# Products of a constant tile at the start, eight places for raw weight blocks, and four items' exponentials taken from PSUM

## The chip, the cores and the metric

One core of a Trainium2 chip runs the whole program. TensorE multiplies, VectorE (DVE), ScalarE (ACT) and GpSimd (POOL) do the element-wise work, and SyncE (SP) issues the DMA transfers. The metric is the device time of one execution in microseconds; the kernel before takes 992.88 us, the median of 3 runs.

## What is computed

Attention with positive random features, followed by a feed-forward block. The inputs are q, k and v of shape 8 x 8 x 576 x 64 (batch, heads, sequence, head size), omega of 128 x 64, w_in of 512 x 2048 and w_out of 2048 x 512, all float32 (q is drawn 4.675 times wider than k).

```python
def phi(x):
    proj = np.einsum('bhsd,md->bhsm', x, omega)
    sq = np.sum(x * x, axis=-1, keepdims=True) / 2.0
    h = proj - sq
    h = h - np.max(h, axis=-1, keepdims=True)
    return np.exp(h) / np.sqrt(m)
q_p, k_p = (phi(q_s), phi(k_s))
kv = np.einsum('bhsm,bhsd->bhmd', k_p, v)
z = np.sum(k_p, axis=2)
num = np.einsum('bhsm,bhmd->bhsd', q_p, kv)
den = np.einsum('bhsm,bhm->bhs', q_p, z)[..., None] + 1e-06
...
h = x @ w_in
sp = np.where(h > 20.0, h, np.log1p(np.exp(np.minimum(h, 20.0))))
g = h * np.tanh(sp)
return (g @ w_out).astype(np.float32)
```

q_s and k_s are q and k over the fourth root of 64, and x is the attention output laid out as 4608 tokens of 512. Since the square term is the same for all features of a row, the subtraction of the row's maximum takes it away.

## The kernel before

**Items.** The attention is cut into 68 items. A key item (`k_task`) is one batch and two of its heads: the keys times omega (`pk`, nine tiles of 128 x 128), the row maxima, the exponentials `e`, and their product with the values (`pkv`). A query item (`q_task`) is 128 tokens of all eight heads: `pq`, maxima, exponentials, a transpose, and the product with the keys' result (`pn`). The order begins with the four key items of batch 0 (items 0 to 3), four query items (4 to 7), the four key items of batch 1 (8 to 11) and the fifth query item (12). These thirteen are computed in float32 throughout ("whole" in the code); all later ones split each operand into two float16 parts and make three products. `features` (L294 to L344) does what both kinds share: a PSUM tile from the pool `ps_a` (four places) for each group of up to four tiles, a reduction for the maxima, and the exponentials into a buffer `e` (two places).

**Maxima and exponentials.** For the items numbered below 9, ACT takes the exponential straight from PSUM, one instruction for each 128 x 128 tile, with the negated maximum as bias (L332). From item 9 on, VectorE subtracts the maxima from PSUM into `e` (L336) and ACT then takes one exponential over all of `e` (L342). Which it is follows from the table `ROLE` by the entry `sub="AD"`: A below item 9, D from there.

**Weights.** w_in comes as eight raw blocks of 1 MB of 64-bit words (a float32 pair each, so that the low and high halves can be taken apart), fetched by `fetch_w` (L137 to L149). A `w_task` (L160 to L182) then unpacks each: a Prelu on ACT (L169), a shift (L170), an or (L174) and a reduction for the block's largest value (L177) on VectorE. When all eight maxima are there, the scale follows (`am_w`, L190), and `w_split` (L198 to L209) makes the two float16 parts. The raw blocks of w_in take turns in four places inside the tile `wo`, so block 4 to 7 can be fetched only once block 0 to 3 is unpacked; w_out's blocks go to two places in `wo` and to buffers of the tag "g" (four places), which the first key loads and the feed-forward activations also use. The split of w_out later overwrites `wo`.

**Feed-forward.** Tokens go through in 18 chunks of 256. Chunk 0 is done in float32 on the unpacked, unscaled weights (`ph` at L609, then `po` at L669); the later ones take three float16 products (L609, L652).

**What sets the order.** The program is written as generators on an agenda; a step counter runs on, and a task resumes at its due step. `FIRST` holds the steps at which the first 18 items start, `WIS` those of the eight w_in blocks, `WOS` those of w_out, and `PREL` the loads that are issued before everything else. Each engine then executes its own queue in order, and so does SP with the transfers that it issues. A scheduling layer places the instructions into the queues, so a change in one place can shift neighbours on all engines. Transfers that wait for a free place hold up those behind them on SP.

Of the kernel before, what the change touches and what calls it, by code (L numbers as in the profile page):

```python
# [9 lines left out]
F16 = mybir.dt.float16  # L10
F32 = mybir.dt.float32
# [3 lines left out]
AF = mybir.ActivationFunctionType  # L15
# [14 lines left out]
def tile_kernel(  # L30
# [10 lines left out]
    nc = tc.nc  # L41
    P = 128
    NT, D, H, _ = qT.shape
    B, HP, _, _, S = kT.shape
# [12 lines left out]
    const = ctx.enter_context(tc.tile_pool(name="const", bufs=1))  # L57
    sb = ctx.enter_context(tc.tile_pool(name="sb", bufs=2))
    ps_h = ctx.enter_context(tc.tile_pool(name="ps_h", bufs=2, space=PSUM))
    ps_o = ctx.enter_context(tc.tile_pool(name="ps_o", bufs=2, space=PSUM))  # L60
    ps_a = ctx.enter_context(tc.tile_pool(name="ps_a", bufs=4, space=PSUM))

    act, dve, pool = nc.scalar, nc.vector, nc.gpsimd
# [19 lines left out]
    lnt = const.tile([P, 1], F32, name="lnt")  # L83
    dve.memset(lnt, LNT)

    ident = const.tile([P, P], F32, name="ident")
    make_identity(nc, ident)

# [48 lines left out]
    def fetch_w(n, i, dma):  # L137
        src = w_src[n](i)


        at = i % 4 if n == 0 else {7: 0, 6: 1, 3: 0}.get(i)
        if at is not None:
            if n == 0 and i >= 4:
                must(1, "w", 0, i - 4)
            raw = wo_t[:, 2 * at:2 * at + 2].rearrange("p a b c -> p (a b c)").bitcast(I64)
        else:
            raw = sb.tile([P, BW], I64, tag="g", name=f"raw{i}", bufs=GB)
        dma.dma_start(out=raw.rearrange("p (a b) -> p a b", b=src.shape[2]), in_=src)
        return raw  # L149
# [8 lines left out]
    def w_task(i, name):  # L158

        n = 0 if name == "wi" else 1  # L160
        raw = loaded.pop(f"w{n}_{i}", None) or fetch_w(n, i, w_dma)
        yield W_LOAD
        word = raw.bitcast(I32).rearrange("p (n two) -> p n two", two=2)
        low, high = word[:, :, 0], word[:, :, 1]
        dst = flat32(slots[w_at(n, i)])
        di = dst.bitcast(I32)
        with behind((AN, AO)[n][i]):
            m = high.bitcast(F32)
            act.activation(m, m, AF.Prelu, scale=2.0 ** -112, alpha=-(2.0 ** 32))  # L169
            dve.tensor_single_scalar(out=di, in_=low, scalar=29, op=ALU.logical_shift_right)  # L170
        yield W_GAP
        did("w", n, i)
        with behind((AN, AO)[n][i]):
            dve.scalar_tensor_tensor(  # L174
                out=di, in0=high, scalar=3, in1=di, op0=ALU.logical_shift_left, op1=ALU.bitwise_or
            )
            dve.tensor_reduce(  # L177
                out=wmax[n][:, i:i + 1], in_=dst, axis=AX.X, op=ALU.max, apply_absolute_value=True
            )
# [37 lines left out]
    def must(n, *key):  # L217
        assert done.get(key, 0) >= n, key
# [57 lines left out]
    kv = {}  # L276
# [5 lines left out]
    def fetch(load, name, tag="af", bufs=2):  # L282
        f = sb.tile([D, load.shape[1] * load.shape[2]], F32, tag=tag, name=f"f{name}", bufs=bufs)
        nc.sync.dma_start(out=f.rearrange("d (a b) -> d a b", b=load.shape[2]), in_=load)
        return f

    def in_parts(f, name, nth):

        ks = sb.tile([P, f.shape[1]], F16, tag="as", name=f"s{name}", bufs=2)
        cast(by("hi", nth), ks[0:D], f)  # L290
        yield gap("hi", name)
        rest(by("lo", nth), ks[D:P], f, ks[0:D])
        yield gap("lo", name)
        return (ks, om[:, 1, :]), (ks, om[:, 0, :])  # L294

    def features(load, tiles, name, nth, whole):

        f = loaded.pop(name, None) or fetch(load, name)  # L300
        yield gap("load", name)
        if whole:

            terms = ((f, om_f[0:D]),)
        else:
            terms = yield from in_parts(f, name, nth)
        n = sum(len(g) for g in tiles)
        by_act = by("sub", nth) is act
        e = sb.tile([P, n, M], F32, tag="ae", name=f"e{name}", bufs=2)
        mx = sb.tile([P, n], F32, tag="mx", name=f"mx{name}")  # L310
        pps, lo = [], 0
        for g in tiles:
            pp = ps_a.tile([P, 4, M], F32, tag="a", name=f"p{name}_{lo}")
            for i, parts in enumerate(g):
                for rows, o in parts:
                    for j, (left, right) in enumerate(terms):
                        nc.tensor.matmul(  # L317
                            out=pp[rows, i, :], lhsT=left[:, o:o + rows.stop - rows.start],
                            rhs=right, start=j == 0, stop=j == len(terms) - 1,
                        )  # L320
            pps.append((pp, lo, lo + len(g)))
            lo += len(g)
        yield 1
        for pp, lo, hi in pps:
            m = hi - lo
            sub = dve.tensor_reduce(  # L326
                out=mx[:, lo:hi], in_=pp[:, :m, :], axis=AX.X, op=ALU.max, negate=by_act
            )
            if by_act:
                assert whole  # L330
                for i in range(m):
                    last = act.activation(  # L332
                        e[:, lo + i, :], pp[:, i, :], AF.Exp, bias=mx[:, lo + i:lo + i + 1]
                    )
            else:
                sub = dve.tensor_tensor(  # L336
                    out=e[:, lo:hi, :], in0=pp[:, :m, :],
                    in1=mx[:, lo:hi].unsqueeze(2).broadcast_to([P, m, M]), op=ALU.subtract,
                )
        yield gap("exp", name)  # L340
        if not by_act:
            last = act.activation(e, e, AF.Exp, bias=0.0 if whole else lnt)  # L342
        anchors[nth] = (last.ins, sub.ins)
        return e  # L344

# [19 lines left out]
    def k_task(nth, b, hp):  # L365
        if hp == 0:
# [7 lines left out]
            [[(rows, S + t * P)] for t in range(4)],  # L374
        ]
        e = yield from features(kT[b, hp], tiles, f"k{b}_{hp}", nth, b < KF)
        dst = kv[b][:, 2 * hp:2 * hp + 2]
        steps = [[(4 * j + i, 5 * j + i) for i in range(5)] for j in range(2)]
# [59 lines left out]
    def q_task(nth, t):  # L438
# [3 lines left out]
        rows = slice(0, P)  # L442
        tiles = [[[(rows, (4 * g + i) * P)] for i in range(4)] for g in range(2)]
        e = yield from features(qT[t], tiles, f"q{t}", nth, t < QF)
        if t < QF:
            yield from q_first(nth, t, e, off)
# [241 lines left out]
    w_dma = nc.sync  # L688

    FIRST = (0, 1, 2, 3, 4, 4, 9, 9, 19, 21, 24, 27, 32, 36, 43, 58, 59, 68)  # L690
    WIS = (4, 5, 6, 7, 9, 11, 12, 13)
    WOS = (28, 27, 26, 25, 24, 23, 22, 21)
    WI0, FF0, V0, V1 = 0, 17, 0, 16
    W_LOAD, W_GAP, PRIO = 1, 1, 400
# [3 lines left out]

    W_LO = ('dddddddd', 'dddddddd')
    W_HI = ('aaaaaaaa', 'aaaaaaaa')  # L700
    PREL = "k0 k2 k1 k3 q0 q1 w0 v w1 w2 w3"
    KF, QF = 2, 5
    GAP0 = {'load': 1, 'exp': 0, 'kv': 1}
    GAP = {'load': 3, 'hi': 1, 'lo': 2, 'exp': 1, 'kv': 2}

    ROLE = dict(hi="AA", lo="PP", sub="AD", kp="AA", kplo="DD", v="DD", vlo="PP", kv="AA", x="AD", xlo="DP", h="DD", h0="DD", gm="DD", g="DA", glo="PD")
    NE, CE = 9, 3
    ENG = {"A": act, "D": dve, "P": pool}

    def gap(what, name):  # L710
        if name in ("k0_0", "k0_1", "k0_2", "k0_3", "q0", "q1"):
            return GAP0[what]
        return GAP[what]
# [5 lines left out]
    def by(role, nth):  # L719
        return ENG[ROLE[role][nth >= NE]]  # L720

    def by_c(role, c):
        if c == 0 and role[0] == "h":
            return act
        return ENG[ROLE[role][c >= CE]]

# [6 lines left out]
    def start(gen, after=0):  # L733
        agenda.append([slot[0] + after, gen])
# [24 lines left out]
    for t in range(NT):  # L759
        last = (t * P + P - 1) // S  # L760
# [29 lines left out]

    for what in PREL.split():
        i = int(what[1:] or 0)
        if what[0] == "k":
            loaded[f"k0_{i}"] = fetch(kT[0, i], f"k0_{i}", *(("af", 2) if i < 2 else ("g", GB)))
        elif what[0] == "q":
            loaded[f"q{i}"] = fetch(qT[i], f"q{i}", "xT", 3)
        elif what[0] == "v":
            for hp in range(HP):
                loaded[f"v0_{hp}"] = fetch_v(0, hp)
        else:  # L800
            loaded[f"w0_{i}"] = fetch_w(0, i, nc.sync)
# [3 lines left out]
    for i in range(NB):  # L805
        start(w_task(i, "wi"), WIS[i])
    for i in reversed(range(1, NB)):
# [83 lines left out]
```

## Time and profile before

| | us |
|---|---|
| median of 3 runs | 992.88 |
| lowest, highest | 992.82, 995.17 |
| the profiled execution | 983.8 |
| its span, first to last instruction | 982.0 |

The page's second part cuts the span into 40 slices and gives the busy tenths of each engine (9 is 90% or more), the granted TensorE clock, and the DMA engines' share; a slice is 24.6 us.

```profile
PE   7999998889999999999999999999999999999998
DVE  4579979688576565656556654655555645211110
ACT  3368656757687777787766875787776776232230
PEclk9999999999999999999999999999999999999999
DMA  9376423542352245223422246322421034200000
```

VectorE is lightly used in the first slices and nearly full from the third to the seventh; the DMA engines are full in the first. In the rows of the timeline that the prediction shows, a row gives the start, the length, the engine, the line, the operation, out<-in, the form, and the number of instructions merged into it; in brackets stands the idle time ahead of it and what ended that. A float32 product counts as two records on TensorE.

### The profile page before, as it was taken

How to read it: one execution, taken by the hardware profiler on the slowest of the kernel's cores; microseconds unless marked ns; L12 is line 12 of the kernel's file. 1: busy time of each engine (PE TensorE's matmuls, PEld its weight loads, DVE VectorE, ACT ScalarE, POOL GpSimd, SP SyncE). 2: the span in 40 equal slices, each digit the busy share in tenths (PEclk: the TensorE clock that was granted, in tenths of full speed). 3: DMA queues.
4: the chain of work that ended last, by engine and by line, in shares of the span. 5: the costliest groups of instructions: out<-in, count | busy, mean ns of one | idle time of the engine just before them, and what ended most of it. 6: DMA issues, size and time to landing. Idle time of an engine off the chain costs nothing.

```text
span 982.0 us, 19120 instructions
## 1 busy us (share of the span) xinstructions
PE 958.3 (98%) x8144; PEld 692.1 (70%) x8144; DVE 552.4 (56%) x974; ACT 625.8 (64%) x783; POOL 219.1 (22%) x135
## 2 busy tenths in 40 slices
PE   7999998889999999999999999999999999999998
PEld 6988775567767777777777777777767777666663
DVE  4579979688576565656556654655555645211110
ACT  3368656757687777787766875787776776232230
POOL 0000013234333322332222332332232230000000
PEclk9999999999999999999999999999999999999999
DMA  9376423542352245223422246322421034200000
GB/s 291 119 246 216 144 57 70 101 86 82 74 122 69 60 96 106 67 55 99 94 62 58 61 102 100 68 57 66 89 67 42 25 76 86 44 22 12 12 11 33
DMA packets 122245, 82.21 MB, mean 84 GB/s; under 512 B 102832, under 2 KB 102960, under 8 KB 122160
## 3 DMA queue, kind: packets, MB, share of 16 engines
q1 hardware_dynamic: 122160, 80.99, 33.1%
q8 instruction: 64, 1.05, 0.4%
q14 instruction: 21, 0.17, 0.1%
HBM read 46.37 MB, written 9.44 MB: 57 GB/s over the span
## 4 chain that ended last, share of the span: by engine, by line
PE 72%; DMA 0%; ACT 0%; DVE 0%; issue 0%; ACTq 0%; SPq 0%
PE po L652 32%; PE ph L609 30%; PE pk L317 3%; PE pq L317 2%; PE pn L468 2%; PE pkv L418 2%; DMA qp<-qn 0%; DVE qn L77 0%; ACT eq L342 0%; ACT qn L68 0%; ACT o L68 0%; ACTq L68 0%; SPq L454 0%
## 5 line engine op out<-in xcount | busy, mean ns | idle before, releaser
L609 PE MATMUL ph<-xT,w 128*128 128x256 f16 (+1 forms) x3392 | 409.8, 277 | 1.0 <-ACT g L68 1.0
L652 PE MATMUL po<-wo,g 128*128 128x512 f16 x1632 | 373.8, 379 | 0.0
L609 PEld LDWEIGHTS <-w 128*128 128x128 f16 x3264 | 317.3, 98 | 59.2 <-issue 0.7
L652 PEld LDWEIGHTS <-g 128*128 128x128 f16 x1632 | 155.6, 98 | 163.6 <-issue 0.4
L628 ACT ACTIVATE h<-ph,us 128x512 f32<-128x512 f32 (+3 forms) x184 | 101.0, 574 | 190.5 <-PE ph L609 189.6
L79 DVE SCALAR_TENSOR_TENSOR g<-h,us,g 128x1024 f16<-128x1024 f32 (+3 forms) x92 | 113.9, 1253 | 119.6 <-ACT g L68 119.3
L77 POOL TENSOR_TENSOR sq<-fq,sq 64x1024 f16<-64x1024 f32 x31 | 71.4, 2303 | 201.0 <-issue 87.5
L77 POOL TENSOR_TENSOR sk<-fk,sk 64x1152 f16<-64x1152 f32 x24 | 60.5, 2522 | 125.4 <-ACT sk L68 27.0
L326 DVE TENSOR_REDUCE mxq<-pq 128x4 f32<-128x512 f32 x72 | 46.8, 683 | 53.2 <-PE pq L317 53.2
L77 POOL TENSOR_TENSOR xs<-x,xs 128x512 f16<-128x512 f32 x32 | 42.4, 1324 | 142.3 <-ACT h L628 56.4
L68 ACT ACTIVATE g<-h,us 128x1024 f16<-128x1024 f32 (+3 forms) x80 | 72.5, 932 | 1.2
L628 ACT ACT_TABLE_LOAD x56 | 71.8, 1283 | 1.0
L342 ACT ACT_TABLE_LOAD x56 | 71.8, 1283 | 1.0
L326 DVE TENSOR_REDUCE mxk<-pk 128x4 f32<-128x512 f32 (+1 forms) x96 | 50.4, 550 | 36.3 <-PE pk L317 36.0
L77 DVE TENSOR_TENSOR qn<-eq,qn 128x1024 f16<-128x1024 f32 x31 | 42.4, 1366 | 48.6 <-ACT qn L68 48.4
L77 DVE TENSOR_TENSOR kp<-ek,kp 128x1152 f16<-128x1152 f32 x24 | 37.2, 1550 | 19.2 <-ACT kp L68 19.2
L77 POOL TENSOR_TENSOR vb<-vf,vb 128x640 f16<-128x640 f32 x24 | 39.8, 1662 | 26.8 <-DVE vb L70 18.4
L68 ACT ACTIVATE o<-po,us 128x512 f32<-128x512 f32 (+1 forms) x38 | 25.9, 681 | 30.2 <-PE po L652 30.1
L342 ACT ACTIVATE eq<-eq,lnt 128x1024 f32<-128x1024 f32 x31 | 35.6, 1149 | 13.6 <-DVE eq L336 13.1
L265 DVE TENSOR_REDUCE vmx<-vf 128x1 f32<-128x640 f32 x32 | 25.6, 814 | 30.1 <-DMA vf<-in_vL_dram 30.1
L336 DVE TENSOR_TENSOR ek<-pk,mxk 128x512 f32<-128x512 f32 (+1 forms) x81 | 42.2, 549 | 0.4
L336 DVE TENSOR_TENSOR eq<-pq,mxq 128x512 f32<-128x512 f32 x64 | 41.2, 680 | 0.0
(112 smaller groups left out, 928.2 us busy)
## 6 DMA issues: line engine op xcount, KB each, us to landing
vf<-in_vL_dram SPq DMA_DIRECT2D x32, 325.0 KB, 3.3
fk<-in_kT_dram SPq DMA_DIRECT2D x32, 288.0 KB, 3.7
fq<-in_qT_dram SPq DMA_DIRECT2D x36, 256.0 KB, 3.5
out_dram<-o SPq DMA_DIRECT2D x36, 256.0 KB, 2.3
wo<-in_w_in_dram SPq DMA_DIRECT2D x8, 1024.0 KB, 10.3
raw<-in_w_out_dram SPq DMA_DIRECT2D x5, 1024.0 KB, 5.9
wo<-in_w_out_dram SPq DMA_DIRECT2D x3, 1024.0 KB, 7.6
xT<-xs SPq DMA_TRANSPOSE x34, 3.1
```

Of the source, the lines that this page charges most:

```text
L68: act.activation(out, in_, AF.Copy, scale=scale)
L77: eng.tensor_tensor(out=out, in0=in_, in1=hi, op=ALU.subtract)
L79: eng.scalar_tensor_tensor(out=out, in0=in_, scalar=scale, in1=hi, op0=ALU.mult, op1=ALU.subtract)
L265: dve.tensor_reduce(out=mx[:, hp:hp + 1], in_=vt[hp][:, :, 0:D], axis=AX.XY, op=ALU.max, apply_absolute_value=True,)
L317: nc.tensor.matmul(out=pp[rows, i, :], lhsT=left[:, o:o + rows.stop - rows.start], rhs=right, start=j == 0, stop=j == len(terms) - 1,)
L326: sub = dve.tensor_reduce(out=mx[:, lo:hi], in_=pp[:, :m, :], axis=AX.X, op=ALU.max, negate=by_act)
L336: sub = dve.tensor_tensor(out=e[:, lo:hi, :], in0=pp[:, :m, :], in1=mx[:, lo:hi].unsqueeze(2).broadcast_to([P, m, M]), op=ALU.subtract,)
L342: last = act.activation(e, e, AF.Exp, bias=0.0 if whole else lnt)
L418: nc.tensor.matmul(out=pkv[:, j, :], lhsT=kp[:, x, t, :], rhs=vv[:, y, u, :], start=i == 0, stop=i == len(mm) - 1,)
L609: nc.tensor.matmul(out=ph[:, i, :], lhsT=wi(a, k, f) if c else wi0(k, f), rhs=xT[c][:, y, k, :] if c else xT0()[:, k, :], start=n == 0, st ...
L628: act.activation(h[:, :, lo:hi], ph[:, :, lo:hi], AF.Mish, scale=us[:, 0:1])
L652: nc.tensor.matmul(out=po[i], lhsT=gT[c, gr][:, a, f % FG, i * P:(i + 1) * P], rhs=wo(y, f), start=f == 0 and (a, y) == parts[0], stop=f = ...
```

## The change

Four edits. A tile `idle` of ones (128 x 512, float16) is written by VectorE, and a helper `spin` multiplies into a PSUM tile that nobody reads. Sixteen such products of `idle` with itself stand ahead of everything else on TensorE, and after each of the items 0 to 5 two products of the identity with the first two tiles of that item's exponentials. The raw blocks 4 to 7 of w_in no longer take turns in `wo` but go to buffers of the tag "g", so all eight have a place; `PREL` fetches all eight ahead of the first steps, and `WIS` starts their unpacking earlier. And the items 9 to 12 take their exponentials straight from PSUM like the ones before them, so that the entry `sub` falls away.

```diff
+    idle = const.tile([P, 512], F16, name="idle")
+    dve.memset(idle, 1.0)
+
+    def spin(n, left, right):
+        pi = ps_o.tile([P, 512], F32, tag="o", name=f"spin{nc.next_id()}")
+        for _ in range(n):
+            nc.tensor.matmul(out=pi[:, 0:right.shape[1]], lhsT=left, rhs=right, start=True, stop=True)
+
+    spin(16, idle[:, 0:P], idle)
...
-        at = i % 4 if n == 0 else {7: 0, 6: 1, 3: 0}.get(i)
+        at = ({0: 0, 1: 1, 2: 2, 3: 3}, {7: 0, 6: 1, 3: 0})[n].get(i)
         if at is not None:
-            if n == 0 and i >= 4:
-                must(1, "w", 0, i - 4)
...
-        by_act = by("sub", nth) is act
+        by_act = whole
...
-                assert whole
...
         if not by_act:
-            last = act.activation(e, e, AF.Exp, bias=0.0 if whole else lnt)
+            last = act.activation(e, e, AF.Exp, bias=lnt)
+        elif nth < 6:
+            spin(2, ident, e[:, 0:2, :].rearrange("p n m -> p (n m)"))
...
-    WIS = (4, 5, 6, 7, 9, 11, 12, 13)
+    WIS = (3, 4, 5, 6, 7, 8, 9, 10)
...
-    PREL = "k0 k2 k1 k3 q0 q1 w0 v w1 w2 w3"
+    PREL = "k0 k2 k1 k3 q0 q1 w0 v w1 w2 w3 w4 w5 w6 w7"
...
-    ROLE = dict(hi="AA", lo="PP", sub="AD", kp="AA", ...
+    ROLE = dict(hi="AA", lo="PP", kp="AA", ...
```

The first place where rows move is the start of TensorE's queue. A row is one instruction, or several alike with their count; `pk_0_0` is item 0's first group of key products, `pkv_0` its product with the values. Before:

```order
L317 MATMUL pk_0_0_148<-om_f,fk_0_105 128x128 x4
L317 MATMUL pk_0_4_153<-om_f,fk_0_105 64x128 x2
L317 MATMUL pk_0_5_156<-om_f,fk_0_105 128x128 x4
L317 MATMUL pk_1_0_175<-om_f,fk_1_109 128x128 x4
L317 MATMUL pk_1_4_180<-om_f,fk_1_109 64x128 x2
L317 MATMUL pk_1_5_183<-om_f,fk_1_109 128x128 x4
L386 MATMUL pkv_0_188<-vf_0_118,ek_0_146 128x65 x10
```

And in the changed kernel, from the last of the sixteen products on:

```order
L93 LDWEIGHTS idle
L93 MATMUL spin_75<-idle 128x512
L326 MATMUL pk_0_0_176<-om_f,fk_0_125 128x128 x4
L326 MATMUL pk_0_4_181<-om_f,fk_0_125 64x128 x2
L326 MATMUL pk_0_5_184<-om_f,fk_0_125 128x128 x4
L326 MATMUL pk_1_0_207<-om_f,fk_1_129 128x128 x4
L93 MATMUL spin_202<-ek_0_174,ident 128x256 x2
L326 MATMUL pk_1_4_212<-om_f,fk_1_129 64x128 x2
L326 MATMUL pk_1_5_215<-om_f,fk_1_129 128x128 x4
L93 MATMUL spin_244<-ek_1_205,ident 128x256 x2
L396 MATMUL pkv_0_220<-vf_0_138,ek_0_174 128x65 x10
```

The order of the items' own products is kept; item 0's spins stand inside item 1's key products, and item 1's directly ahead of item 0's product with the values. The spins of items 2 and 3 stand behind the pkv of items 1 and 2, those of items 4 and 5 around the first transposes.

The second place is SP's queue of loads behind the first values (`vf`). Before, with the blocks of w_in as `wo`, the queries of items 6 and 7 as `fq`, and the values and keys of batch 1:

```order
L255 DMA vf_3_124<-in_vL_dram 128x650
L148 DMA wo<-in_w_in_dram 128x4x256 x4
L284 DMA fq_439<-in_qT_dram 64x1024
L284 DMA fq_441<-in_qT_dram 64x1024
L148 DMA wo<-in_w_in_dram 128x4x256 x3
L255 DMA vf_0_608<-in_vL_dram 128x650
```

In the changed kernel the blocks 4 to 7 are the `raw` rows:

```order
L264 DMA vf_3_144<-in_vL_dram 128x650
L157 DMA wo<-in_w_in_dram 128x4x256 x3
L157 DMA raw_149<-in_w_in_dram 128x4x256
L157 DMA raw_151<-in_w_in_dram 128x4x256
L157 DMA raw_153<-in_w_in_dram 128x4x256
L157 DMA raw_155<-in_w_in_dram 128x4x256
L293 DMA fq_496<-in_qT_dram 64x1024
L293 DMA fq_498<-in_qT_dram 64x1024
L264 DMA vf_0_656<-in_vL_dram 128x650
```

Three blocks move ahead of the two queries; the last two raw rows take the buffers of the first batch's third and fourth key loads.

The third place is VectorE's queue at item 9, the second key item of batch 1 (`mxk_1` its maxima, `ek_1` its exponentials, `w_88` a block of w_in that is split, `wo` a block of w_out that is unpacked). Before:

```order
L326 TENSOR_REDUCE mxk_1_707<-pk_1_0_708 128x4
L326 TENSOR_REDUCE mxk_1_707<-pk_1_4_713 128x1
L336 TENSOR_TENSOR ek_1_706<-pk_1_0_708,mxk_1_707 128x512
L336 TENSOR_TENSOR ek_1_706<-pk_1_4_713,mxk_1_707 128x128
L326 TENSOR_REDUCE mxk_1_707<-pk_1_5_716 128x4
L79 SCALAR_TENSOR_TENSOR w_88<-w_89,s_w_593,w_88 128x1024
L336 TENSOR_TENSOR ek_1_706<-pk_1_5_716,mxk_1_707 128x512
L174 SCALAR_TENSOR_TENSOR wo<-raw_694,wo 128x1024
```

In the changed kernel:

```order
L335 TENSOR_REDUCE mxk_1_755<-pk_1_0_756 128x4
L335 TENSOR_REDUCE mxk_1_755<-pk_1_4_761 128x1
L335 TENSOR_REDUCE mxk_1_755<-pk_1_5_764 128x4
L79 SCALAR_TENSOR_TENSOR w_108<-w_109,s_w_641,w_108 128x1024
L183 SCALAR_TENSOR_TENSOR wo<-raw_742,wo 128x1024
```

The three subtractions are gone, and the rows around them stay in their order.

More of the change, by code (lines that the diff above doesn't have):

```diff
@@ L704, in tile_kernel @@
     GAP = {'load': 3, 'hi': 1, 'lo': 2, 'exp': 1, 'kv': 2}
-    ROLE = dict(hi="AA", lo="PP", sub="AD", kp="AA", kplo="DD", v="DD", vlo="PP", kv="AA", x="AD", xlo="DP", h="DD", h0="DD", gm="DD", g="DA", glo="PD")
+    ROLE = dict(hi="AA", lo="PP", kp="AA", kplo="DD", v="DD", vlo="PP", kv="AA", x="AD", xlo="DP", h="DD", h0="DD", gm="DD", g="DA", glo="PD")
     NE, CE = 9, 3
```

## The prediction

> **What bounds the kernel now.** I read the page's busy table and chain first, then the timeline of TensorE, then busy time by stretch, then the queue of the loads.
>
> ```profile
> PE 958.3 (98%) x8144; PEld 692.1 (70%) x8144; DVE 552.4 (56%) x974; ACT 625.8 (64%) x783; POOL 219.1 (22%) x135
> PE 72%; DMA 0%; ACT 0%; DVE 0%; issue 0%; ACTq 0%; SPq 0%
> 0.00:54.00 54.00, 46.70 (x207) 42.20 (x207) 23.73 (x40) 21.90 (x63) 1.66 (x15) 1.00 0.69 219
> 54.00:128.00 74.00, 72.47 (x451) 60.63 (x451) 68.01 (x116) 51.49 (x78) 1.43 (x3) 0.98 0.55 183
> 128.00:162.00 34.00, 33.72 (x262) 25.32 (x260) 26.57 (x62) 22.79 (x28) 7.34 (x6) 1.00 0.15 40
> 162.00:215.00 53.00, 42.92 (x347) 27.84 (x347) 40.34 (x65) 33.45 (x39) 17.83 (x10) 0.97 0.51 102
> 215.00:982.00 767.00, 762.48 (x6885) 536.08 (x6882) 393.79 (x693) 496.15 (x580) 190.85 (x104) 1.00 0.29 65
> ```
>
> TensorE is busy for 98% of the span and carries the chain. After 215 us it idles 4.5 us in all, and its order there is set beforehand, so what it gains before 215 should reach the end whole. The rows by stretch give the busy time of TensorE, its weight loads, VectorE, ACT and GpSimd, then the granted clock, the DMA share and GB/s. They also show where something else is close: VectorE is busy 68.0 of 74 us from 54 to 128, and TensorE idles 10.1 us from 162 to 215. So the question is how early TensorE can leave the first 54 us, and whether the rest follows. A busy TensorE need not be a fast one, so I compared equal products at different places:
>
> ```profile
> 5.11 8.99 PE L317 MATMUL pk<-om_f,fk 64*128 64x128 f32 x40 [5.11 <-DMA fk<-in_kT_dram]
> 15.51 4.50 PE L386 MATMUL pkv<-vf,ek 128*128 128x65 f32 x20 [1.41 <-DVE w L170]
> 29.02 4.69 PE L317 MATMUL pk<-om_f,fk 64*128 64x128 f32 x20
> 38.10 7.19 PE L317 MATMUL pq<-om_f,fq 64*128 64x128 f32 x32
> 45.22 4.53 PE L386 MATMUL pkv<-vf,ek 128*128 128x65 f32 x20
> 49.55 1.06 PE L511 MATMUL pt<-ident,eq 128*128 128x128 f32 x4
> 51.29 3.31 PE L511 MATMUL pt<-ident,eq 128*128 128x128 f32 x12 [0.69 <-ACT qp L68]
> 54.39 3.83 PE L522 MATMUL pn<-kvf,qp 128*128 128x65 f32 x32
> ...
> 79.45 2.61 PE L317 MATMUL pk<-om_f,fk 64*128 64x128 f32 x20
> 107.86 2.34 PE L386 MATMUL pkv<-vf,ek 128*128 128x65 f32 x20
> 133.19 2.05 PE L317 MATMUL pq<-om_f,fq 64*128 64x128 f32 x16
> 141.11 1.09 PE L511 MATMUL pt<-ident,eq 128*128 128x128 f32 x8 [0.20 <-ACT eq L342]
> ```
>
> The same twenty records of pk take 4.69 us early and 2.61 us late, those of pkv 4.53 and 2.34 us. Everything up to about 54 us runs at half pace. The column of the granted clock shows 1.00 for that stretch (its first row above), so it does not report this state and the durations must. Loads are not the reason:
>
> ```profile
> 40.00:50.00 10.00, 10.00 (x48) 9.78 (x48) 7.83 (x9) 3.50 (x10) 0.00 (x0) 1.00 0.16 44
> 95.69 2.45 PE L386 MATMUL pkv<-vf,ek 128*128 128x65 f32 x20
> 99.10 2.93 PE L609 MATMUL ph<-xT,w 128*128 128x256 f32 x6 [0.96 <-ACT g L68]
> 86.72 7.17 PE L609 MATMUL ph<-xT,w 128*128 128x256 f32 x32
> 95.00:100.00 5.00, 4.04 (x29) 0.91 0.69 209
> 100.00:110.00 10.00, 10.00 (x59) 0.88 0.42 153
> ```
>
> The last two rows are TensorE's alone (busy, clock, DMA). From 40 to 50 us the DMA engines are at 16% and pkv still takes 4.53 us. The second to fourth rows tell what the pace follows: after narrow products (65 columns wide) and 0.96 us of idling, the wide ph takes 0.49 us a record for about 3 us instead of 7.17/32 = 0.22, and there the granted clock does dip. So the clock falls when the array is thinly used (64 of 128 rows, or 65 columns a weight load), even while TensorE counts as busy, and comes back after some 3 us of full-width work. At the start that came only with the transposes pt at 49 to 54 us.
>
> The Trainium skill, "TensorE: Matmul & The Clock Gate", section "What's actually happening", says that the clock is half until one window of about 3.4 us of sustained activity and full afterwards. By that rule pk at 5.11 us would have opened the clock by about 9 us; this trace has it at half pace through 30 us of unbroken products (19.94 to 49.75), so here the measurement decides.
>
> **The change, part by part.** *Products ahead of the first keys.* Sixteen f16 products of 512 columns start when the constant is written, 1.0 to 1.7 us (bounds: the first DVE write ends near 0.85 us; a four times wider one than ident's 0.20 us lies ahead).
>
> ```profile
> 187.81 2.75 PE L652 MATMUL po<-wo,g 128*128 128x512 f16 x12
> 15.40 0.82 DVE L265 TENSOR_REDUCE vmx<-vf 128x1 f32<-128x640 f32 x1
> 0.72 0.20 POOL masks.py:197 MEMSET ident<- 128x128 f32 x1 [0.29 <-POOLq L878]
> ```
>
> One costs 2.75/12 = 0.23 us at full clock, twice that at half: sixteen end between 4.7 and 9.0 us. That is at least 16 x 0.23 = 3.7 us of full width, more than the 2.93 us of ph at 99.10 or the 3.3 us of pt after which the clock was back, so they should open it. Two pk at full pace (5.2 us) and two pairs of spins (below, 1.8 us) then end between 11.7 and 16.0 us. The next product, pkv of item 0, needs the first values, which land at about 15.4 us (the DVE row that starts on them); the loads ahead of them are unchanged. So everything before 15.4 us is covered, by 0 to 3.7 us of waiting, and at worst 0.6 us is not.
>
> *The stretch from 15.5 us to the first pn (54.39).* Now 38.9 us. At full pace: four pkv 4 x 2.34 = 9.4, two pk 5.2, pq 2 x 2.05 = 4.1, four groups of pt 2.2; together 20.9, so 18.0 us go.
>
> *Spins between items.* Each is two f32 products of 256 columns, four records of ph's form, 4 x 0.22 = 0.9 us at full clock and 4 x 0.49 = 2.0 at half. Six pairs; those of items 0 and 1 lie in the wait above, four are on TensorE's path: 3.6 us. They write PSUM places that nothing uses before 120 us.
>
> *New waits.* At twice the pace TensorE meets the exponentials: item 5's may only be written once item 3's pkv has read its buffer (two buffers), and cost 1.14 us for four before the transposes can go. Bounds: 0, and 4 us if each of the four last items waits as item 5 does; I take 1.1, nearest to the 0.69 us that pt waited so far.
>
> Sum for this stretch: 18.0 - 3.6 - 1.1 = **13.3 us**.
>
> *Eight places.* The last three raw blocks of w_in were held back for a place until 35 to 50 us:
>
> ```profile
> 9.53 9.12 SPq L148 DMA_DIRECT2D wo<-in_w_in_dram x4
> 35.60 14.81 SPq L148 DMA_DIRECT2D wo<-in_w_in_dram x3
> 20.00:30.00 10.00, 10.00 (x45) 9.10 (x45) 4.14 (x11) 3.69 (x12) 0.38 (x1) 1.00 1.02 346
> 58.76 0.66 DVE L170 TENSOR_SCALAR w<-wo 128x1024 int32<-128x1024 int32 x1
> 73.84 0.15 DVE L190 TENSOR_REDUCE am_w<-wmax 128x1 f32<-128x8 f32 x1
> ```
>
> All eight now queue at once; at 346 GB/s the last 4.2 MB take 12 us, so they are in by about 38 us. The loads for items 6 and 7 move behind two of them on the DMA queue, to about 38 us; their products are due near 46, so 8 us cover that. Two blocks wait on that queue for pk of items 2 and 3, which TensorE has then done by about 26 us. The direct gain is nothing on TensorE, but it is the cover of the 13.3 us: VectorE unpacked blocks 4 to 7 from 58.76 to 73.84 us because they came late, and it was idle for 30 of the first 54 us. Without the early blocks most of the gain would be handed back there.
>
> *Exponentials of items 9 to 12.* Eleven subtractions leave VectorE.
>
> ```profile
> L336 DVE TENSOR_TENSOR ek<-pk,mxk 128x512 f32<-128x512 f32 (+1 forms) x81 | 42.2, 549 | 0.4
> L336 DVE TENSOR_TENSOR eq<-pq,mxq 128x512 f32<-128x512 f32 x64 | 41.2, 680 | 0.0
> 93.05 2.43 ACT L332 ACTIVATE ek<-pk,mxk 128x128 f32<-128x128 f32 x9
> 103.02 1.15 ACT L342 ACTIVATE ek<-ek 128x1152 f32<-128x1152 f32 x1
> 134.38 0.69 DVE L326 TENSOR_REDUCE mxq<-pq 128x4 f32<-128x512 f32 x1 [6.38 <-PE pq L317]
> ```
>
> Nine at 0.549 and two at 0.680: 6.3 us. ACT pays 2.43 instead of 1.15 us for each of three key items and about as much for the query: 4.9 us, beside TensorE, since ACT is busy 51.5 of the 74 us to 128; without that cover 4.9 us would be the price. What VectorE saves is needed: its 68.0 us of work from 54 to 128 become 61.7, and TensorE's demand at 134.38, for which VectorE then idled 6.38 us, comes 13.3 us earlier. That leaves 80.4 - 13.3 = 67 us for 61.7: 92%, the same density as now (68.0/74). It should fit, with nothing to spare; I count 0, bounds 0 and -4.
>
> **The sum.** 983.8 us (the profiled execution, span 982.0 and 1.8 around it) less 13.3 gives 970.5. The median of the runs is 992.88, 9 us above the profiled one; I carry the gain over as it is: 992.9 - 13.3 = 979.6, say **980 us**, own range 974 to 986.
>
> **Rivals.** *The clock falls back and recovers.* The wait for the values at up to 15.4 us is idle time of up to 3.7 us, followed by narrow pkv; 0.96 us beside pkv was enough at 99 us. Half pace from about 16 us until the pair after item 2 has run, some 13 us, loses 6.5: 986. Against it: the pairs of items 0 and 1 stand right ahead of that wait. The Trainium skill, same page, section "Why this matters for your kernels", asks only for no idle gaps over about 3 us; by that rule most of these waits would be harmless, by the row at 99.10 us a shorter one was not, and I go by the row.
>
> *It falls back and stays, and the change is slower.* If a pair in half-clock time is too little to open it, four pairs cost 4 x 2.0 = 7.8 us on TensorE's path, the products keep their old durations, and only about 1 us of the first pkv is saved: 992.9 + 6.8 = 1000. It decides where 2 us of full width in some 11 us do not count as activity. For it: twelve pt, 3.3 us, were needed. Against: clusters of spins and pt around items 4 and 5.
>
> *The half pace is no clock at all* but belongs to the first stage. Then the change adds 3.6 us of pairs and about 2 us ahead: 998. By the page's rule above this would be so, since the clock would be open from 9 us; the dip at 99 us and the equal halving of four kinds of product speak against.
>
> *Given back later.* TensorE comes earlier, but VectorE at 92% or the transposed queries do not:
>
> ```profile
> PE pn L468 <- DMA qp<-qn: 10.8, 4, 3.7
> ```
>
> These waits end with a chain of VectorE, ACT and a transfer; if the two that follow the first chunk grow by 3 us each and VectorE lags a little: 987.
>
> *Nothing on balance*, new waits and lag together eating the gain: 992. *More*: if the timed runs, 9 us above the profiled one, stay at half pace longer than it did, the gain is nearer 22 us: 971.
>
> **Chances.** Forecast 0.50, falls back and recovers 0.17, given back 0.10, more 0.08, nothing 0.05, stays and slower 0.06, no clock 0.04. The range 970 to 992 leaves out the two slower cases, half of "nothing" and part of "more": under 0.2. Faster or slower means by over 0.3%, 3 us, about what a measurement here can tell from no change: faster (under 989.9) 0.49 + 0.14 + 0.08 + 0.08 + 0.01 = 0.80; slower 0.06 + 0.04 = 0.10; the same 0.10.
>
> **What would show it.** Right: pkv of items 0 to 3 near 2.4 us each and pk near 2.6; the first pn near 41 us instead of 54.39; the last block of w_in on SP's queue before 30 us; VectorE's idling before 54 us much less than 30 us; the maximum over w_in (73.84) about 13 us earlier. Wrong: pkv at 4.5 us after 16 us, spin records at 0.49 us, a granted clock that dips between 10 and 40 us, or TensorE's idle time in the stretch that is 54 to 215 us now grown beyond its 11.9 us (1.5 to 128 us, 0.3 to 162, 10.1 to 215).

## The result: 2.5% faster

| | before, us | changed, us | ratio, 95% interval |
|---|---|---|---|
| first measurement | 993.2 (4 runs) | 968.7 (4 runs) | 0.9744 (0.9719 to 0.9770) |
| repeat on another chip | 992.6 (12 runs) | 967.9 (4 runs) | 0.9748 (0.9731 to 0.9765) |

The gain is 24.5 us where 13 were forecast, and 968.7 us lies below the range of 970 to 992. The medians here and below are over all runs, while the ratios leave out runs more than 1.5% above the fastest of their kernel, here one of 5616 us with products several times longer from end to end. The profile below is that of the repeat (967.9 us, span 966.0).

The busy times of the whole span and the stretches of the changed kernel, with columns as in the prediction:

```profile
PE 951.4 (98%) x8184; PEld 681.4 (71%) x8184; DVE 543.6 (56%) x964; ACT 627.5 (65%) x812; POOL 219.2 (23%) x135
15.00:54.00 39.00, 36.36 (x258) 32.88 (x258) 33.61 (x57) 23.06 (x58) 0.38 (x1) 0.91 0.79 268
54.00:128.00 74.00, 73.92 (x496) 61.43 (x495) 59.72 (x117) 59.54 (x108) 2.60 (x4) 0.98 0.51 164
128.00:162.00 34.00, 29.07 (x189) 19.32 (x188) 27.07 (x44) 21.42 (x24) 16.20 (x8) 0.95 0.33 78
162.00:215.00 53.00, 52.54 (x462) 35.57 (x461) 37.43 (x64) 37.06 (x45) 17.73 (x9) 1.00 0.40 86
47.20:57.40 10.20, 10.20 (x40) 9.35 (x41) 9.98 (x15) 1.15 (x4) 0.35 (x1) 0.50 0.53 162
```

TensorE's busy total shrinks by 7 us although 40 records were added: the same products became shorter. VectorE now works in the first stage (33.6 of the 39 us from 15 to 54, where it had 19.5 before). But the granted clock is not 1.00 everywhere: from 47.2 to 57.4 us it is 0.50. TensorE's timeline of the changed kernel shows both (`spin` are the added products, `px` the transposes of the attention output x for the feed-forward block):

```profile
1.47 5.95 PE L93 MATMUL spin<-idle 128*128 128x512 f16 x16 [1.47 <-DVE idle L88]
7.35 3.50 PE L326 MATMUL pk<-om_f,fk 64*128 64x128 f32 x28
...
13.29 1.13 PE L93 MATMUL spin<-ek,ident 128*128 128x256 f32 x4
15.27 2.42 PE L396 MATMUL pkv<-vf,ek 128*128 128x65 f32 x20 [0.85 <-DMA vf<-in_vL_dram]
17.62 2.61 PE L326 MATMUL pk<-om_f,fk 64*128 64x128 f32 x20
...
33.05 2.45 PE L396 MATMUL pkv<-vf,ek 128*128 128x65 f32 x20
35.33 1.08 PE L93 MATMUL spin<-eq,ident 128*128 128x256 f32 x4
...
39.55 3.68 PE L532 MATMUL pn<-kvf,qp 128*128 128x65 f32 x32
45.34 0.44 PE L556 MATMUL px<-ident,x 128*128 128x128 f32 x2 [1.02 <-DVE x L539]
46.46 0.70 PE L619 MATMUL ph<-xT,w 128*128 128x256 f32 x2 [0.69 <-ACT xT L68]
47.09 7.15 PE L326 MATMUL pq<-om_f,fq 64*128 64x128 f32 x32
```

pkv takes 2.4 us and pk 2.6 us from the start, as forecast, and the first pn begins at 39.55 us instead of 54.39: 14.8 us earlier, for 13.3 worked out. Then two short waits at px and ph are followed by pq at half pace, 7.15 us instead of some 3.8. Against the profiled execution of before (983.8 us) the gain is 15.9 us. The other 9 us have to come from a difference between executions of the kernel before.

### The profile page after: what moved, and what is told of

Read it like the earlier page. It is cut to its first block, busy times and chain, and to the rows that moved or that the text cites. A ratio compares the mean times of both kernels' runs of the same rounds, so it can differ in the third digit from the quotient of the medians.

```text
span 5614.3 us, 19216 instructions
## 1 busy us (share of the span) xinstructions
PE 5607.3 (100%) x8184; PEld 2589.2 (46%) x8184; DVE 561.4 (10%) x964; ACT 637.0 (11%) x812; POOL 217.6 (4%) x135
## 4 chain that ended last, share of the span: by engine, by line
PE 100%; ACT 0%; DVE 0%; issue 0%; ACTq 0%
PE ph L619 42%; PE po L662 38%; PE pk L326 4%; PE pq L326 4%; PE po L679 3%; PE pn L478 2%; PE pkv L428 2%; PE pkv L396 2%; PE spin L93 1%; PE pn L532 1%; PE pt L521 0%; PE px L556 0%; ACT o L68 0%; ACT xT L68 0%; DVE idle L88 0%
## 5 line engine op out<-in xcount | busy, mean ns | idle before, releaser
L619 PE MATMUL ph<-xT,w 128*128 128x256 f16 (+1 forms) x3392 | 2380.7, 1071 | 0.7 <-ACT xT L68 0.7
L662 PE MATMUL po<-wo,g 128*128 128x512 f16 x1632 | 2201.1, 1703 | 0.0
L619 PEld LDWEIGHTS <-w 128*128 128x128 f16 x3264 | 1050.4, 322 | 1216.1 <-issue 1215.8
L662 PEld LDWEIGHTS <-g 128*128 128x128 f16 x1632 | 520.3, 321 | 1411.1 <-issue 1407.0
L326 PE MATMUL pq<-om,sq 128*128 128x128 f16 x496 | 175.3, 713 | 0.0
L326 PEld LDWEIGHTS <-sq 128*128 128x128 f16 x496 | 145.7, 320 | 39.5 <-issue 22.5
L326 PE MATMUL pk<-om,sk 128*128 128x128 f16 (+1 forms) x480 | 152.3, 645 | 0.0
L679 PE MATMUL po<-wo,g 128*128 128x512 f32 x56 | 149.9, 3022 | 0.0
L478 PEld LDWEIGHTS <-qp 128*128 128x128 f16 (+1 forms) x816 | 134.4, 262 | 31.7 <-issue 31.7
L478 PE MATMUL pn<-kv,qp 128*128 128x65 f16 (+1 forms) x816 | 136.8, 470 | 0.0
## 6 DMA issues: line engine op xcount, KB each, us to landing
raw<-in_w_in_dram SPq DMA_DIRECT2D x4, 1024.0 KB, 10.1
```

The source lines that it names most:

```text
L326: nc.tensor.matmul(out=pp[rows, i, :], lhsT=left[:, o:o + rows.stop - rows.start], rhs=right, start=j == 0, stop=j == len(terms) - 1,)
L478: nc.tensor.matmul(out=pn[lo:hi, i, :], lhsT=qp[:, a, h, lo:hi], rhs=kv[b][:, h, y, :], start=n == 0, stop=n == 2,)
L619: nc.tensor.matmul(out=ph[:, i, :], lhsT=wi(a, k, f) if c else wi0(k, f), rhs=xT[c][:, y, k, :] if c else xT0()[:, k, :], start=n == 0, st ...
L662: nc.tensor.matmul(out=po[i], lhsT=gT[c, gr][:, a, f % FG, i * P:(i + 1) * P], rhs=wo(y, f), start=f == 0 and (a, y) == parts[0], stop=f = ...
L679: nc.tensor.matmul(out=po[i], lhsT=g0(f // FG)[:, f % FG, i * P:(i + 1) * P], rhs=wo0(f), start=blk == NB - 1 and f % 2 == 0, stop=blk == ...
```

## The experiments

**The kernel before, profiled again.**

> The kernel before, once more, with a profile. Theory A with a varying moment of the clock: this execution takes about 993 us and stays at half pace beyond 54.7 us, to about 65 to 75 us, where the profile shown so far (983.8 us) left it at 54.7. Rival (a fixed offset between profiled and plain executions): it takes 984 us and the pace doubles near 54 us as before.

It took 992.71 us, and its timeline from the transposes on reads as follows; below it stands the second pn in the execution of the prediction:

```profile
49.57 1.06 PE L511 MATMUL pt<-ident,eq 128*128 128x128 f32 x4
51.32 3.31 PE L511 MATMUL pt<-ident,eq 128*128 128x128 f32 x12 [0.69 <-ACT qp L68]
54.42 6.93 PE L522 MATMUL pn<-kvf,qp 128*128 128x65 f32 x32
61.15 1.54 PE L546 MATMUL px<-ident,x 128*128 128x128 f32 x6
...
70.65 6.71 PE L609 MATMUL ph<-xT,w 128*128 128x256 f32 x22
77.20 0.60 PE L511 MATMUL pt<-ident,eq 128*128 128x128 f32 x4
80.25 3.69 PE L522 MATMUL pn<-kvf,qp 128*128 128x65 f32 x32
```

```profile
71.47 3.69 PE L522 MATMUL pn<-kvf,qp 128*128 128x65 f32 x32
```

From the first pkv at 15.5 us up to 54.42 us it is the execution of the prediction, to 0.03 us. Then pn takes 6.93 us instead of 3.83, and 3.69 the next time. The clock did not open at the transposes but only within ph; the first record of the granted clock in this trace is a rise at 74.1 us, in the other one at 54.7. The second pn begins 8.8 us later (80.25 for 71.47), which is nearly all of the 8.9 us between the two spans. So the profile that the prediction used was of an execution in which the half pace ended 19 us sooner than in this one. Of the 65 runs of the kernel before that accompany the experiments, 16 lie between 982.6 and 985.5 us and all others at 990.9 or above; the faster group is a quarter of them.

**The changed kernel again**, without an edit.

> The changed kernel once more, for a profile in the ordinary state. Theory A (clock): TensorE's early products run at full pace, pkv of items 0 to 3 near 2.4 us and pk near 2.6 us, the first pn near 41 us; time 967 to 970 us. Theory B (the gain came mostly from VectorE's relief and the earlier blocks): pkv still near 4.5 us at least to 40 us, and the gain shows between 54 and 215 us as fewer TensorE waits.

967.9 us, the profile shown above. Theory A holds: pkv, pk and the first pn are where it puts them. Between 128 and 162 us TensorE idles 4.9 us where it idled 0.3 before, and between 162 and 215 us 0.5 where it idled 10.1, so waits have moved as well as shrunk.

**Spins alone.** The kernel before plus the helper and its two uses:

```diff
+    spin(16, idle[:, 0:P], idle)
...
+        elif nth < 6:
+            spin(2, ident, e[:, 0:2, :].rearrange("p n m -> p (n m)"))
```

> The kernel before plus the sixteen products and the six pairs, nothing else. Theory A: most of the gain is here, 970 to 980 us, short of the whole change because VectorE gets blocks 4 to 7 late. Theory B: within 5 us of the kernel before, or slower by the 3.6 us of the pairs.

961.6 us, ratio 0.9669 (0.9640 to 0.9697): better than the whole change, and better than either theory expected. Its TensorE and its stretch from 15 to 54 us:

```profile
39.49 3.69 PE L534 MATMUL pn<-kvf,qp 128*128 128x65 f32 x32
...
44.19 1.83 PE L327 MATMUL pq<-om_f,fq 64*128 64x128 f32 x14
45.95 0.44 PE L558 MATMUL px<-ident,x 128*128 128x128 f32 x2
46.32 2.27 PE L327 MATMUL pq<-om_f,fq 64*128 64x128 f32 x18
```

```profile
15.00:54.00 39.00, 38.12 (x287) 34.30 (x288) 33.65 (x57) 27.35 (x73) 0.38 (x1) 1.00 0.89 301
```

The first pn comes at the same moment as in the whole change. Here pq fills the wait for x between the transposes px, and the clock stays at 1.00. VectorE does as much from 15 to 54 us (33.65 us) as with eight places (33.61): beside a faster TensorE it unpacks sooner, and the old places come free sooner (the last three blocks of w_in are issued from 26.64 us on instead of 35.60).

**No spins.** The changed kernel without the constant tile, the sixteen products and the pairs.

```diff
-    spin(16, idle[:, 0:P], idle)
...
-        elif nth < 6:
-            spin(2, ident, e[:, 0:2, :].rearrange("p n m -> p (n m)"))
```

> The changed kernel without the sixteen products and without the pairs: eight places and the exponentials alone. Theory A: 987 to 993 us, since TensorE stays at half pace to 54 us or longer and is what bounds that stretch. Theory B: 970 to 978 us.

990.1 us, ratio 0.9974 (0.9946 to 1.0001). Eight places and the exponentials alone bring at most 0.5%. Theory A holds, Theory B falls.

**Which of the two other edits costs.** Each was taken away by itself. Spins and exponentials, with the old places (the kernel of spins alone and this):

```diff
-        by_act = by("sub", nth) is act
+        by_act = whole
```

> The kernel before plus all spins plus the exponentials of items 9 to 12 from PSUM, but with the old four places. Theory P (the eight places cost what separates 968 from 962 us: they put VectorE's unpacking ahead of x, TensorE waits at px near 45 us, and the clock falls there): 957 to 962 us, no dip of the clock near 47 us. Rival E (ACT's longer exponentials cost it): 966 to 970 us.

963.8 us, ratio 0.9741 (0.9686 to 0.9796). The time lies between the two forecasts and decides nothing by itself; the trace does, since pq again stands around px and the clock does not fall there. Spins and eight places, with the subtraction back:

```diff
-        by_act = whole
+        by_act = by("sub", nth) is act
```

> The changed kernel with the exponentials of items 9 to 12 as before (subtraction on VectorE), all spins and the eight places kept. Theory P: 967 to 972 us with a clock dip near 47 us. Rival E: 960 to 963 us.

971.1 us, ratio 0.9809 (0.9753 to 0.9865), as Theory P has it, with the same fall (half clock from 48.1 us on, for 10.2 us):

```profile
45.39 0.44 PE L557 MATMUL px<-ident,x 128*128 128x128 f32 x2 [1.02 <-DVE x L540]
46.52 0.70 PE L620 MATMUL ph<-xT,w 128*128 128x256 f32 x2 [0.69 <-ACT xT L68]
47.15 6.39 PE L326 MATMUL pq<-om_f,fq 64*128 64x128 f32 x32
```

So the loss sits with the eight places and the earlier fetches that go with them, which were not taken apart: with the spins and no other edit the ratio is 0.9669 (0.9640 to 0.9697), with the places added 0.9809, clear of each other. The exponentials' own effect has no clear sign: beside the old places the kernel with them is slower by its ratio (0.9741 for 0.9669), beside the new ones faster (0.9748 for 0.9809), with overlapping intervals in both pairs.

**Filling that wait.** Two pairs more, which read x and so stand between the transposes px, added to the whole change:

```diff
             nc.tensor.transpose(out=px[:, i, :], in_=x[:, 2 * i:2 * i + 2, :], identity=ident)
+        spin(2, ident, x[:, 0:4, :].rearrange("p h d -> p (h d)"))
```

> The changed kernel plus two pairs of the same products between the transposes px of the first two query items, in the place where TensorE waits 1.0 us for x and 0.7 us for xT; they read x. If the eight places cost their 6 us through the clock that falls at 47 us: no dip at 47 us, pq of items 6 and 7 near 3.9 us for 32 records instead of 7.1, time 962 to 965 us. If VectorE's order itself costs it: 968 to 970 us.

963.6 us, ratio 0.9703 (0.9666 to 0.9741), and the mean granted clock rises from 0.993 to 0.998 in four of its six runs. These four lie at 962.6 to 964.2 us, seven of the eight of the changed kernel, on other chips, at 967.2 to 970.0; the medians of the kernel before beside them differ by 0.6 us at most. So 4.3 of the some 6 us come back by adding work that computes nothing, and most of what the eight places cost was the clock and not the order of VectorE. The one profile of this kernel is that of the run of 1106 us and cannot show the place; that the fall at 47 us is gone rests on the time and the mean clock. The same edit on the kernel with spins alone:

> The same two pairs added to the kernel before with the spins alone, where the clock did not fall there. If the clock is what matters: they only cost, 0 to 2 us over the spins alone, but runs with a fall of the clock become rarer. A gain over 2 us would speak for something else.

961.1 us, ratio 0.9684 (0.9646 to 0.9722): no gain where there was no fall, as expected. And the spins alone once more:

> The kernel before plus all spins, again: 957 to 963 us if its lead of 6 us over the whole change holds on this chip, 966 or more if it was the first chip's or chance.

The median is 968.6 us, which is the second forecast, and the ratio 0.9684 (0.9638 to 0.9730) over three runs at 958.8 to 962.5 us, which is the first. The other three lay at 975 to 982 us with a mean clock of 0.974 to 0.981 instead of 0.996, some 30 to 45 us of additional half pace. One of four runs had been of this kind the first time, one of six with the pairs at px, and one each with the exponentials (981.6), with the eight places (990.2) and with the whole change and the pairs at px (981.9); of the eight runs of the whole change none was, apart from the one of 5616 us. So the lead of the spins alone is one of the faster runs, not of every run.

**Half the rows.** Every spin on 64 of the 128 rows:

```diff
-    spin(16, idle[:, 0:P], idle)
+    spin(16, idle[0:D, 0:P], idle[0:D, :])
...
-            spin(2, ident, e[:, 0:2, :].rearrange("p n m -> p (n m)"))
+            spin(2, ident[0:D, :], e[0:D, 0:2, :].rearrange("p n m -> p (n m)"))
```

> The changed kernel with every spin on 64 of the 128 rows (half of the constant tile, of the identity and of the exponentials): same count, same columns, same time on TensorE. If the clock follows how much of the array is used: it stays at half pace, pkv near 4.5 us up to 45 us, and the time is 985 to 1000 us. If only busy time or streamed columns count: 967 to 970 us as before.

995.7 us, ratio 1.0069 (1.0035 to 1.0102):

```profile
1.47 7.01 PE L93 MATMUL spin<-idle 64*128 64x512 f16 x16 [1.47 <-DVE idle L88]
8.28 6.24 PE L326 MATMUL pk<-om_f,fk 64*128 64x128 f32 x28
20.48 4.53 PE L396 MATMUL pkv<-vf,ek 128*128 128x65 f32 x20
53.63 4.53 PE L396 MATMUL pkv<-vf,ek 128*128 128x65 f32 x20
```

The same number of products of the same width keeps TensorE just as busy and does not open the clock. Of the two theories, the one that counts how much of the array is used holds, and the spins at half pace now only cost: 5.6 us over the kernel without spins.

**Sixteen without pairs, pairs without the sixteen.** The changed kernel, each time with the other use of `spin` taken out (the diff of no spins, one half at a time).

> The changed kernel with the sixteen products ahead but without the pairs between items. If the pairs are what holds the clock up through the narrow products: the clock opens near 6 us and falls again between 15 and 30 us, time 974 to 988 us. If the first sixteen suffice: 963 to 966 us, faster by the pairs' 3.6 us.

> The changed kernel without the sixteen products ahead, pairs kept. By what the clock needed so far (a window of some 3.4 us filled by 0.7 or more with full-width products): one pair beside narrow products at half pace fills about 0.7, so it opens at the first pair that falls whole into a window, between 14 and 35 us; time 968 to 978 us. If only the sixteen can open it: 990 to 996 us.

990.3 us, ratio 0.9993 (0.9953 to 1.0034), and 990.9 us, 0.9982 (0.9961 to 1.0004). Neither does anything by itself. The first three rows are from the timeline of the sixteen alone, the last two from that of the pairs alone; the two between are stretches of the sixteen alone (TensorE busy, granted clock, DMA):

```profile
1.47 5.54 PE L93 MATMUL spin<-idle 128*128 128x512 f16 x16 [1.47 <-DVE idle L88]
6.95 4.95 PE L326 MATMUL pk<-om_f,fk 64*128 64x128 f32 x40
15.34 4.50 PE L394 MATMUL pkv<-vf,ek 128*128 128x65 f32 x20 [3.44 <-DMA vf<-in_vL_dram]
```

```profile
5.50:12.00 6.50, 6.40 (x47) 1.00 1.02 220
12.30:56.00 43.70, 39.29 (x175) 0.50 0.73 254
```

```profile
11.42 2.07 PE L91 MATMUL spin<-ek,ident 128*128 128x256 f32 x4
37.73 4.53 PE L393 MATMUL pkv<-vf,ek 128*128 128x65 f32 x20
```

The sixteen open the clock, and it falls again at 12.2 us, at the end of pk and 0.3 us into the wait for the values. The time that pk saves goes into that wait, which is 3.44 us instead of 1.20 without spins. The pairs did not open the closed clock among the narrow products of the items 0 to 3: two products, 2 us, are too little there. Where they stand as well, as in the changed kernel, the clock that the sixteen opened stays up. Both forecasts of a middle time were wrong: 974 to 988 us for the sixteen, whose clock also fell sooner than the 15 to 30 us named, and 968 to 978 us for the pairs.

**Two pairs and nothing else.** Whether the kernel before varies by the moment at which its clock opens was still an inference from two traces. So only the pairs of items 4 and 5, around the first transposes, were added to it:

```diff
+        elif nth in (4, 5):
+            spin(2, ident, e[:, 0:2, :].rearrange("p n m -> p (n m)"))
```

> The kernel before plus nothing but the two pairs of items 4 and 5, which stand around the first transposes; with pt they make some 7 us of full-width products without a gap. If the kernel before lies near 992 us because its clock mostly does not open at pt (54.7 us) but only in ph (74 us): here it opens near 56 to 60 us every time, all runs lie at 983 to 987 us, and none at 991 or above. If the 9 us between the two groups of its runs have another cause: the runs stay divided, most of them at 992 to 996 us.

983.4 us, ratio 0.9946 (0.9913 to 0.9978). Ten of twelve runs lie between 981.9 and 985.1 us, two at 988.5 and 989.6, which the forecast did not have, none above; of the 17 runs of the kernel before beside them, 11 lie at 990.9 to 997.4.

```profile
49.35 2.02 PE L90 MATMUL spin<-eq,ident 128*128 128x256 f32 x4
52.01 1.06 PE L90 MATMUL spin<-eq,ident 128*128 128x256 f32 x2
53.35 0.60 PE L90 MATMUL spin<-eq,ident 128*128 128x256 f32 x2
54.89 3.69 PE L531 MATMUL pn<-kvf,qp 128*128 128x65 f32 x32
```

pn takes 3.69 us, and the clock opened at 52.95 us, sooner than the 56 to 60 us named. Four products that compute nothing move the typical run into the faster group: with the two traces above, this is where the missing 9 us were.

**Three products an item**, on the spins alone with the pairs at px:

```diff
-            spin(2, ident, e[:, 0:2, :].rearrange("p n m -> p (n m)"))
+            spin(3, ident, e[:, 0:2, :].rearrange("p n m -> p (n m)"))
```

> The kernel before plus all spins, three instead of two products after each of the items 0 to 5, and the two pairs at px. Four of the added products lie on TensorE's path, 4 x 0.45 = 1.8 us: 962 to 964 us, and if the executions at 975 us and above are falls of the clock in the narrow products, none of those.

970.2 us, ratio 0.9781 (0.9720 to 0.9843) where two an item had 0.9684 (0.9646 to 0.9722). Three runs lie at 965 to 967.5 us, two at 973 to 974, and one took 3501 us. The forecast of 962 to 964 us missed. No other run lies at 975 us or above, but falls did not go away: the profile (974.0 us) catches one.

```profile
1.47 5.03 PE L92 MATMUL spin<-idle 128*128 128x512 f16 x16 [1.47 <-DVE idle L87]
15.67 2.42 PE L398 MATMUL pkv<-vf,ek 128*128 128x65 f32 x20 [1.31 <-DMA vf<-in_vL_dram]
18.02 4.69 PE L327 MATMUL pk<-om_f,fk 64*128 64x128 f32 x20
22.64 4.53 PE L398 MATMUL pkv<-vf,ek 128*128 128x65 f32 x20
29.11 2.80 PE L92 MATMUL spin<-ek,ident 128*128 128x256 f32 x6
33.70 2.45 PE L398 MATMUL pkv<-vf,ek 128*128 128x65 f32 x20
```

The clock opened early here, at 4.3 us, the sixteen were over by 6.5, and the wait for the values grew to 1.31 us; the clock fell at 18.0 us and came back at 31.6, within the group of six records. That is the forecast's rival "falls back and recovers", with its 13 us, in another kernel. What caused the runs at 975 us and above with two products an item was not profiled; falls of this kind fit their mean clock, but that is not shown.

## Why the prediction was wrong

- **The early half pace, its cause and its cure: right.** pkv at 2.4 us and pk at 2.6 us came as forecast; the clock opened at 6.2 us, 4.7 us after the sixteen products began, and no fall came in the 10 to 40 us that the prediction watched, but one at 47.2. The rival of a half pace that is no clock falls with these durations, and the run on 64 rows shows that being busy is not enough. The Trainium skill, "TensorE: Matmul & The Clock Gate", section "What's actually happening", has the clock at half until about 3.4 us of sustained activity. The sixteen products agree with that; pk, pkv and pq, busy for 30 us at half pace, do not.
- **The stretch to the first pn: right in size.** 13.3 us worked out, 14.8 measured; the new waits there were 0.43 us at pt, not 1.1, and a pair of spins took 0.9 to 1.0 us where 0.9 was assumed.
- **The step that failed: "The median of the runs is 992.88, 9 us above the profiled one; I carry the gain over as it is."** This took the 9 us for a fixed offset. They were a second stretch at half pace: the profiled execution was one of the faster quarter, its clock opened at the transposes (54.7 us), and in the execution of 992.71 us it opened 19 us later, in ph (74.1 us), which moved the second pn by 8.8 us. The spins take that variation away too, so the gain over the median is 15.9 + 9 us. The prediction had this as the rival "more", 971 us, and gave it 0.08. The 0.9% between the profiled and the timed runs, three times the usual scatter, should have carried more weight.
- **After the first pn: near by luck.** That 13.3 us and the 15.9 over the profiled execution are close is partly chance. Of the 14.8 us gained by the first pn, 7.9 were left at pn of items 6 and 7 (71.47 us before, 63.54 in the changed kernel): the waits of 1.0 and 0.7 us and the 10.2 us at half pace took the rest. Behind it 8.1 us came that the sum had at nothing: TensorE's idle time from 54 to 950 us shrank from 12.6 to 5.5 us, its waits for the transposed queries from 10.8 to 1.4, where the rival "given back" let them grow. Why they shrank was not tested. In the typical execution of before this pn begins at 80.25 us, so 16.7 of the 24.9 us between the spans (990.9 and 966.0) lie ahead of it. Of the rest, idle time accounts for 5 (10.7 us before, 5.5 after), and 3.4 fit two fewer short falls of the clock.
- **Eight places: wrong.** I had them as the cover without which most of the gain would be handed back. The kernel without them is faster. In every profiled kernel with them and without pairs at px, pq of items 6 and 7 is placed behind px and the first ph. Nothing is left to fill TensorE's 1.0 and 0.7 us of waiting, and with the spins the clock falls for 10.2 us. The loads of these items now queue behind three more blocks, not two as the prediction has it. They were in time all the same: issued by 29.1 us and at most 14.0 us on their way, they had landed before TensorE fell idle at 44.3. So the fixed order left the gap and not a late load; that the three blocks made the scheduling layer choose this order is likely, but not shown. I had weighed that move by whether the loads come in time, not by what TensorE's order loses.
- **Exponentials: nothing forecast, nothing shown.** VectorE's density was no limit: its 92% between 54 and 128 us became 81% (59.7 of 74), and with the subtractions kept and the spins alone it was 89% (65.65 of 74) in a kernel that was faster still.
- **"Falls back" rivals.** The wait ahead of the first pkv did not bring the clock down in the changed kernel (0.85 us), but together with the narrow pkv it did in the last experiment (1.31 us). Without the pairs the clock fell when the wait had only begun, so there the narrow pk brought it down.

## What to carry to other kernels

Compare the durations of equal products early and late before believing a clock column, and compare the profiled execution's own time with the median: a profile out of the faster group hides part of what a change can gain. Where TensorE's products are narrow, a few full-width ones that compute nothing can be worth more than their time: here some 13 us of them, most of it in waits, for 31 us (992.6 to 961.6). But they work only as a chain: enough in a row to open the clock, then one group in each wait or narrow stretch so that it does not fall. By the ratio the best kernel here is the one before with the spins alone (0.9669, then 0.9684), but four of its ten runs lay at 975 to 982 us, and what made them so stays open; with the pairs at px it was one of six (0.9684). A further edit that looks free must be asked which short TensorE waits it leaves uncovered.

## What the runs showed of the hardware

- **The clock answers to how full the array is, in pieces of 3.41 us.** Every fall lasted 3.4, 6.8 or 10.2 us or another multiple. For each piece of the first 215 us in fourteen traces (all but those of 5616 and 1106 us) I added up the time in which columns stream, about 0.22 us for 256 float32 columns at full pace and twice that at half, as in ph, weighted by the share of the 128 rows in use. At half pace no piece at 0.70 or less opened the clock, all from 0.75 did; the pieces between do not tell where the border lies. At full pace no piece above 0.39 lost it, all below 0.37 did. At half pace a piece of pq alone, on 64 rows, gives 0.50 and one of pkv alone 0.48 (65 columns stream in about half of the 4.53/20 us of a record): too little to open. A piece of pkv at full pace with a microsecond of idling gives 0.32, which is the fall at 99 us, and the one with the two waits at px 0.26, which is the fall at 47 us.
- **Where the pieces begin differs between executions**, so the same queue can open the clock at the transposes (0.81 of the piece from 51.28 us in the trace of the prediction) or miss it (0.62 and 0.60 in the pieces from 50.22 and 53.64 us of the typical one). That the kernel before has its two groups of times from this is inferred from these two traces and the run with two pairs; an estimate from the typical trace agrees: with the pieces shifted to every position, a piece of 0.75 or more comes by 58 us in 18% of them, one of 0.72 or more in 27%, and 16 of the 65 runs, 25%, are in the faster group.
- **Short waits are enough.** Waits of 1.0 and 0.7 us among narrow products were followed by 10.2 us at half pace in the changed kernel. The Trainium skill, "TensorE: Matmul & The Clock Gate", section "Why this matters for your kernels", warns of idle gaps over about 3 us. Here shorter ones were enough.
- **The granted clock says nothing before its first change.** It reads 1.00 for the whole early stage of the kernel before, at half pace.
